# Where a matmul's moving operand starts in a 512-byte row: shifted x operands in a retention and two-MLP kernel

## The chip, the core and the metric

The kernel runs on one core of a Trainium2 chip. The core has a matrix engine (TensorE, PE in the rows, with its weight loads as PEld), a vector engine (VectorE, DVE), a scalar engine (ScalarE, ACT), a general engine (GpSimd, POOL), a queue engine that issues the DMAs here (SyncE, SP), an on-chip memory SBUF of 128 partitions, and PSUM, where matmuls put their sums. The metric is device time of one launch in microseconds (us); less is better.

## What is computed

Retention (attention without softmax, with a decay per head) over 4 batches, 8 heads, 576 positions and 64 dimensions; its output, 2304 tokens of 512 numbers, goes through two MLPs with a hidden width of 2048. All in float32.

```
scores = scale * np.matmul(q, k.transpose(0, 1, 3, 2))
Dmat = np.where(rel >= 0, gamma[:, None, None] ** rel[None, :, :], 0.0)
x = np.matmul(scores * Dmat, v)                  # -> [2304, 512]
h = np.maximum(x @ w_in, 0.0);  x = h * h @ w_out            # first MLP
h = x @ w_in2;  g = h * np.clip(h + 3.0, 0.0, 6.0) / 6.0     # second MLP
out = g @ w_out2
```

## The kernel before

To keep float32 accuracy on a faster matmul type (F32R), every operand is split in a high part and a low rest, and each product is three matmuls: high x high, low x high, high x low. A matmul has a stationary operand (the weights, 128 columns that are loaded into the array first) and a moving operand (its columns stream through). Every matmul of the MLPs has its own weight load.

**First MLP (0 to about 452 us).** The tokens are cut in five blocks of 512, 384, 512, 384 and 512 (`BLOCKS`, L30). A block's x, both parts, is one SBUF tile made by `new_x` (L696): the 512-token blocks 0, 2 and 4 take it from the pool `xapool`, blocks 1 and 3 from `xbpool`. For each block the loop `steps` goes over 16 slices f of the hidden width: `h_part` (L611) does 12 matmuls with weights w and moving operand x (L623), ScalarE and VectorE square the positive part into g, and `a_part` (L645) does 12 matmuls with weights w and moving operand g (L660). Between them stand small matmuls of the retention, which makes the x of later blocks. The weights of all 16 slices stay in SBUF, in the pools `wlo` and `whi`. In the background the second MLP's weights are read, combined, split and written to DRAM (`unit_work`).

**Second MLP (about 452 us to the end).** It uses a seven-product scheme for 2 x 2 blocks of matrices, so its operands are sums and differences, seven of each, named q in the order `ORDER` = 1, 6, 7, 5, 2, 4, 3. The tokens are cut in three passes of 768 (two halves of 384). The seven x operands `x_ops[q]` are SBUF tiles from pool `p1a`, made by `x_tiles` (L791) and filled for each pass by `x_stages`. Weights come from DRAM through a ring of seven SBUF tiles (`ring_load`, L937): six lie in `p1a`, every seventh in `p1c`. Each pass has two layers:

- first layer, L1183: for 8 slices j and 7 operands q, 6 matmuls of 384 columns. Weights: the ring tile. Moving: `x_ops[q]`. 336 matmuls a pass.
- second layer, L1238: for 7 operands q and 8 slices k, 9 matmuls of 256 columns. Weights: the split activation `spl`, one of six tiles, filled by `a_cast` (L1109) and `a_low`. Moving: the ring tile. 504 matmuls a pass. Five of the `spl` tiles lie in `p1a`; the first is a part of an older tile of `upool`, from column `FIRST_SHIFT` on (L1106, L1115).

The order on each engine is written out: in the first MLP by the loop, in the second by a list of due times (`at` and `run`) that only sets the order of issue. What each instruction waits for follows from its tiles.

Where a tile starts in SBUF follows from what its pool has handed out before. `p1a.tile([P, SHIFT])` on L1107 is 64 bytes that nobody uses, ahead of the `spl` tiles; `align` (L108) is another such tile; L1255 fills up behind.

Of the kernel before, what the change touches and what calls it, by code (L numbers as in the profile page):

```python
# [11 lines left out]
F32 = mybir.dt.float32  # L12
F32R = mybir.dt.float32r
# [6 lines left out]
P = 128  # L20
# [5 lines left out]
NC = DM // P  # L26
NF = DFF // P
NCHUNK = NT // P

BLOCKS = [(512, "xa"), (384, "xb"), (512, "xa"), (384, "xb"), (512, "xa")]  # L30


# [2 lines left out]
SUPERS, HALF = 3, 384  # L35
# [51 lines left out]
def retention_moe_kernel(ctx: ExitStack, tc, qk, kv, w1, w2, cst, out):  # L87
# [5 lines left out]
    nc = tc.nc  # L93
    nblk = len(BLOCKS)
    start = np.concatenate([[0], np.cumsum([n for n, _ in BLOCKS])]).tolist()

    def pool(stack, name, bufs, **kw):
        return stack.enter_context(tc.tile_pool(name=name, bufs=bufs, reuse_waits="tile", **kw))
# [97 lines left out]

    n0 = BLOCKS[0][0] // P
    ch = {}
    xs = {}
# [411 lines left out]
    def h_part(ph, blk, f, between=lambda: None):  # L611
        nb = BLOCKS[blk][0]
        w = wts[ph, f, 0]
        x = xs[ph, blk]
        hp = ps_h.tile([P, 512], F32, tag="h", name=f"h_{ph}_{blk}_{f}")
        def order(last):
            return [(c, wi, xi) for wi, xi in ((0, 0), last[::-1], last) for c in range(NC)]

        parts = 2 if ph == blk == f == 0 else 1
        for i in range(parts):  # L620
            ts = slice(i * nb // parts, (i + 1) * nb // parts)
            for k, (c, wi, xi) in enumerate(order((1, 0) if blk == 0 and i == 0 else (0, 1))):
                nc.tensor.matmul(  # L623
                    hp[:, ts],
                    w[:, wi, c * P : (c + 1) * P],
                    x[:, xi, c, ts],
                    start=k == 0,
                    stop=k == 3 * NC - 1,
                )
        r = tmpp.tile([P, 512], F32, tag="tmp", name=f"r_{ph}_{blk}_{f}")  # L630
        r = r[:, :nb]
        nc.scalar.activation(r, hp[:, :nb], AF.Relu)  # L632
        between()
        nc.vector.tensor_tensor(r, r, hp[:, :nb], ALU.mult)  # L634
        g = gpool.tile([P, 2, 512], F32R, tag="g", name=f"g_{ph}_{blk}_{f}")
        nc.scalar.activation(g[:, 0, :nb], r, AF.Copy)  # L636
        gts[ph, blk, f] = g, r

    def g_low(ph, blk, f):
        g, r = gts[ph, blk, f]  # L640
        nb = BLOCKS[blk][0]
        nc.vector.tensor_tensor(g[:, 1, :nb], r, g[:, 0, :nb].bitcast(F32), ALU.subtract)  # L642
        gts[ph, blk, f] = g

    def a_part(ph, blk, f):  # L645
        nb = BLOCKS[blk][0]
        w = wts[ph, f, 1]
        g = gts.pop((ph, blk, f))
        if f == 0:
            two = [  # L650
                ps_acc.tile([P, 2, 512], F32, tag="acc", name=f"acc_{ph}_{blk}_{d}")
                for d in range(2)
            ]
            accs[ph, blk] = [two[d // 2][:, d % 2, :] for d in range(NC)]
        acc = accs[ph, blk]
        last = f == NF - 1

        def mm(d, wi, gi, first, stop):
            wt = w[:, wi, d * P : (d + 1) * P]
            nc.tensor.matmul(acc[d][:, :nb], wt, g[:, gi, :nb], start=first, stop=stop)  # L660

        if last:
            for d in range(NC):
                mm(d, 0, 0, False, False)
                mm(d, 1, 0, False, False)
                mm(d, 0, 1, False, True)
        else:
            for d in range(NC):
                mm(d, 0, 0, f == 0, False)
                mm(d, 1, 0, False, False)  # L670
            for d in range(NC):
                mm(d, 0, 1, False, False)

    p1a = None
# [21 lines left out]
    def new_x(ph, blk):  # L696
        nb, tag = BLOCKS[blk]
        p = xbpool if tag == "xb" else xapool
        xs[ph, blk] = p.tile([P, 2, NC, nb], F32R, tag=tag, name=f"x_{ph}_{blk}")

# [85 lines left out]
    x_ops = {}  # L788
    xpre = None

    def x_tiles(p):  # L791
        for q in ORDER:
            x_ops[q] = p.tile([P, 2, 2, HALF], F32R, tag=f"x{q}", name=f"xop_{q}")

    def x_stages(s):

# [65 lines left out]
    for f in range(2, 4):  # L862
        load_w(0, f)
    nc.sync.dma_start(con, cst[:, DK0:])
    new_x(0, 0)

    first_q(0, nc.vector)
# [98 lines left out]
    for i, (ph, blk, f) in enumerate(steps):  # L966
# [38 lines left out]
        if blk + 1 < nblk:  # L1005
            if f == 0:
                new_x(0, blk + 1)
# [5 lines left out]
        if i == half:  # L1013

            right.close()
            p1a = xpre = pool(ctx, "p1a", 1, side="right")
            x_tiles(p1a)
            x_first = x_stages(0)
            for st in x_first:
                do(st[0])  # L1020
# [35 lines left out]
    def run(t):  # L1056
        while heap and heap[0][0] <= t:
            _, _, fn, a = heapq.heappop(heap)
            fn(*a)  # L1059
# [43 lines left out]

    SHIFT, FIRST_SHIFT = 64 // 4, 192 // 4  # L1106
    p1a.tile([P, SHIFT], F32, tag="shift0", name="shift0")  # L1107

    def a_cast(s, q, k):  # L1109
# [51 lines left out]
    for s in range(SUPERS):  # L1161
# [8 lines left out]
        for j in range(NJ):  # L1170
# [5 lines left out]
            for i, q in enumerate(ORDER):  # L1176
                run(now)
                w = wring[s, 0, j, i // 2][:, i % 2]
                x = x_ops[q]
# [72 lines left out]
            if q not in to:  # L1252
                at(now, merge, q, *{1: (s1, None), 6: (u2, s1), 7: (u3, u2)}[q])
    run(1e9)
    p1a.tile([P, 128 - SHIFT], F32, tag="shift1", name="shift1")  # L1255


# [35 lines left out]
```

## Time and profile before

| | before |
|---|---|
| time, median of 2 runs | 804.15 us (803.68 and 804.63) |
| span of the profiled execution | 802.6 us |
| TensorE busy | 796.4 us, 99% |
| VectorE, ScalarE, GpSimd busy | 592, 398, 168 us |
| first MLP with retention, about | 0 to 452.8 us |
| second MLP: first layers, three stretches | 58.3, 58.2 and 58.3 us |
| second MLP: second layers, three stretches | 57.2, 57.3 and 57.3 us |

The rows come from one profiled execution. Busy time of an engine is the union of its instructions' times; matmuls overlap, each lasting longer than the step from one start to the next, so the step is read from a run of them: the length of the run, without the last one's own duration, over the count less one. In the chain (the work that ended last, followed back from the end) each piece runs from the end of the piece ahead, and its length over its count is the step.

### The profile page before, as it was taken

What the parts mean: (1) busy time and instruction counts of PE and PEld (TensorE: products, weight loads), DVE (VectorE), ACT (ScalarE), POOL (GpSimd) and SP (SyncE); (2) the same over time, 40 slices, a digit from 0 to 9 for tenths busy, and PEclk for the clock granted to TensorE, in tenths of its full rate; (3) what the DMA queues carried; (4) which work ended last, traced back from release to release, by engine and by line L of the source; (5) the groups of instructions that cost most, each with busy time, mean ns of one, the idle gap of its engine ahead of it and who ended that gap; (6) DMA issues with size and microseconds to landing.
All of it is one profiled execution on the core that took longest, in us unless ns stands there. A gap on an engine that the chain in (4) does not pass through costs nothing.

```text
span 802.6 us, 16522 instructions
## 1 busy us (share of the span) xinstructions
PE 796.4 (99%) x6380; PEld 741.0 (92%) x6380; DVE 591.9 (74%) x1086; ACT 397.5 (50%) x738; POOL 167.7 (21%) x161
## 2 busy tenths in 40 slices
PE   8999999999999999999999999999999999999998
PEld 8788889999888899998888899999999999999998
DVE  5989987887755577776557867997577987677864
ACT  2797745444443444444435533666234655244553
POOL 4412130211011011100000065500255500256300
PEclk9999999999999999999999999999999999999999
DMA  9957626777756487856448797888887979877884
GB/s 331 352 189 248 223 93 203 225 214 222 222 157 184 124 260 212 234 158 184 145 130 269 242 303 256 306 307 291 274 264 242 353 261 302 279 240 266 272 274 139
DMA packets 148494, 189.64 MB, mean 236 GB/s; under 512 B 22592, under 2 KB 102080, under 8 KB 148416
## 3 DMA queue, kind: packets, MB, share of 16 engines
q1 hardware_dynamic: 148416, 188.59, 73.5%
q8 instruction: 50, 0.82, 0.4%
q14 instruction: 28, 0.23, 0.1%
HBM read 149.76 MB, written 38.80 MB: 235 GB/s over the span
## 4 chain that ended last, share of the span: by engine, by line
PE 95%; DMA 3%; DVE 1%; SPq 0%; ACT 0%; issue 0%; DVEq 0%
PE acc L660 24%; PE h L623 24%; PE z L1183 22%; PE z L1238 21%; PE at L496 2%; DMA raw<-w_dram 1%; DMA v<-kv_dram 1%; DMA kv<-kv_dram 1%; PE alone L496 0%; PE sc L408 0%; PE o L459 0%; PE sc L419 0%; DVE wt L158 0%; DVE wt L159 0%; PE o L469 0%; ACT w L167 0%
## 5 line engine op out<-in xcount | busy, mean ns | idle before, releaser
L660 PE MATMUL acc<-g,w 128*128 128x512 f32 (+1 forms) x960 | 213.3, 370 | 0.4 <-ACT g L636 0.4
L623 PE MATMUL h<-x,w 128*128 128x512 f32 (+2 forms) x972 | 210.6, 365 | 0.2 <-ACT w L167 0.2
L660 PEld LDWEIGHTS acc<-g,w 128*128 128x128 f32 x960 | 173.6, 188 | 25.2 <-ACT g L636 0.8
L623 PEld LDWEIGHTS h<-x,w 128*128 128x128 f32 x972 | 175.7, 188 | 22.8 <-ACT w L167 0.6
L1183 PE MATMUL z<-xop,ring 128*128 128x384 f32 x1008 | 175.2, 334 | 0.0
L1183 PEld LDWEIGHTS z<-xop,ring 128*128 128x128 f32 x1008 | 174.7, 188 | 0.1
L1238 PE MATMUL z<-ring,spl 128*128 128x256 f32 x1512 | 172.2, 276 | 0.0
L1238 PEld LDWEIGHTS z<-ring,spl 128*128 128x128 f32 x1512 | 172.1, 188 | 0.0
L1099 POOL TENSOR_TENSOR aop<-aop,aop 128x384 f32<-128x384 f32 x96 | 106.2, 1116 | 296.2 <-DVE aop L1096 292.4
L1121 DVE TENSOR_TENSOR spl<-aop,spl 128x384 fp32r<-128x384 f32 x168 | 100.5, 617 | 30.7 <-ACT spl L1117 29.4
L1117 ACT ACTIVATE spl<-aop 128x384 fp32r<-128x384 f32 x168 | 86.3, 523 | 54.7 <-PE z L1238 49.8
L632 ACT ACTIVATE r<-h 128x512 f32<-128x512 f32 (+1 forms) x80 | 44.3, 553 | 110.7 <-PE h L623 110.4
L1093 ACT ACTIVATE aop<-held,small 128x384 f32<-128x384 f32 x72 | 44.4, 617 | 108.4 <-DVE held L1059 107.8
L634 DVE TENSOR_TENSOR r<-r,h 128x512 f32<-128x512 f32 (+1 forms) x80 | 50.5, 632 | 53.9 <-ACT r L632 53.5
L1059 DVE TENSOR_TENSOR held<-z,held 128x384 f32<-128x384 f32 x120 | 66.4, 553 | 28.9 <-PE z L1183 26.7
L636 ACT ACTIVATE g<-r 128x512 fp32r<-128x512 f32 (+1 forms) x80 | 47.2, 590 | 65.8 <-DVE r L634 65.8
L642 DVE TENSOR_TENSOR g<-r,g 128x512 fp32r<-128x512 f32 (+1 forms) x80 | 54.7, 684 | 21.0 <-ACT g L636 18.5
L1096 DVE SCALAR_TENSOR_TENSOR aop<-aop,held 128x384 f32<-128x384 f32 x72 | 49.9, 692 | 17.7 <-ACT aop L1093 16.1
L393 POOL TENSOR_TENSOR qs<-qs,con 128x512 f32<-128x512 f32 x11 | 14.7, 1340 | 136.3 <-DMA qs<-qk_dram 123.9
L750 ACT ACTIVATE uhi<-seven 128x896 fp32r<-128x896 f32 x32 | 30.6, 955 | 23.7 <-DVE seven L740 14.0
L755 DVE TENSOR_TENSOR seven<-seven,uhi 128x896 fp32r<-128x896 f32 x32 | 34.9, 1089 | 7.3 <-ACT uhi L750 7.0
L174 POOL TENSOR_TENSOR w<-wt,w 128x512 fp32r<-128x512 f32 x17 | 22.7, 1336 | 62.9 <-ACT w L167 60.2
(111 smaller groups left out, 609.8 us busy)
## 6 DMA issues: line engine op xcount, KB each, us to landing
ring<-w_out_hl SPq DMA_DIRECT2D x84, 512.0 KB, 4.9
ring<-w_in_hl SPq DMA_DIRECT2D x72, 512.0 KB, 4.7
raw<-w_dram SPq DMA_DIRECT2D x32, 512.0 KB, 7.1
uraw<-w_dram SPq DMA_DIRECT2D x64, 256.0 KB, 3.2
q<-qk_dram SPq DMA_DIRECT2D x17, 512.0 KB, 5.3
w_in_hl<-uhi SPq DMA_DIRECT2D x16, 448.0 KB, 3.4
w_in_hl<-seven SPq DMA_DIRECT2D x16, 448.0 KB, 4.8
w_out_hl<-uhi SPq DMA_DIRECT2D x16, 448.0 KB, 3.2
```

Source lines behind the costliest of these rows:

```text
L623: nc.tensor.matmul(hp[:, ts], w[:, wi, c * P : (c + 1) * P], x[:, xi, c, ts], start=k == 0, stop=k == 3 * NC - 1,)
L634: nc.vector.tensor_tensor(r, r, hp[:, :nb], ALU.mult)
L636: nc.scalar.activation(g[:, 0, :nb], r, AF.Copy)
L642: nc.vector.tensor_tensor(g[:, 1, :nb], r, g[:, 0, :nb].bitcast(F32), ALU.subtract)
L660: nc.tensor.matmul(acc[d][:, :nb], wt, g[:, gi, :nb], start=first, stop=stop)
L1059: fn(*a)
L1096: stt(f32(q, j), f32(q, j), 6.0, h, ALU.min, ALU.mult)
L1099: nc.gpsimd.tensor_tensor(f32(o, j), f32(a, j), f32(b, j), op)
L1117: act(t[:, 0, :], f32(q, k), AF.Copy)
L1121: tt(t[:, 1, :], f32(q, k), t[:, 0, :].bitcast(F32), ALU.subtract)
L1183: nc.tensor.matmul(bank[q], w[:, wi, u * P : (u + 1) * P], x[:, u, xi, :], start=k == 0 and q not in (2, 4, 3), stop=k == 5, skip_group_ch ...
L1238: nc.tensor.matmul(o, sp[:, g, P * n : P * (n + 1)], w[:, k % 2, wi, :], start=k == 0 and m == 0 and n % 2 == 0 and q not in (2, 4, 3), st ...
```

## The change

Nothing is computed differently. Tiles get unused elements, so that operands start at other places in SBUF:

- the x tile of blocks 0, 2 and 4 becomes 128 elements (512 bytes) longer, and x starts in it at element 0, 8 or 120 (`X_PLACE`), which is 0, 32 or 480 bytes on;
- each of the seven x operands of the second MLP becomes 8 elements (32 bytes) longer, so that each starts 32 bytes further in a row of 512 bytes than the one before it, and everything behind them in `p1a` moves by 224 bytes;
- `FIRST_SHIFT` grows by the same 224 bytes, and the filler at the end shrinks by it.

```
+X_PLACE = {0: 0, 2: 8, 4: 120}
     def new_x(ph, blk):
         nb, tag = BLOCKS[blk]
         p = xbpool if tag == "xb" else xapool
-        xs[ph, blk] = p.tile([P, 2, NC, nb], F32R, tag=tag, name=f"x_{ph}_{blk}")
+        n = 2 * NC * nb
+        if tag == "xa":
+            t = p.tile([P, n + P], F32R, tag=tag, name=f"x_{ph}_{blk}")
+            t = t[:, X_PLACE[blk] : X_PLACE[blk] + n]
+            xs[ph, blk] = t.rearrange("p (x c t) -> p x c t", x=2, c=NC)
+        else:
+            xs[ph, blk] = p.tile([P, 2, NC, nb], F32R, tag=tag, name=f"x_{ph}_{blk}")
     def x_tiles(p):
         for q in ORDER:
-            x_ops[q] = p.tile([P, 2, 2, HALF], F32R, tag=f"x{q}", name=f"xop_{q}")
+            t = p.tile([P, 4 * HALF + 8], F32R, tag=f"x{q}", name=f"xop_{q}")
+            x_ops[q] = t[:, : 4 * HALF].rearrange("p (u x t) -> p u x t", u=2, x=2)
-    SHIFT, FIRST_SHIFT = 64 // 4, 192 // 4
+    SHIFT, FIRST_SHIFT = 64 // 4, (192 + 224) // 4
-    p1a.tile([P, 128 - SHIFT], F32, tag="shift1", name="shift1")
+    p1a.tile([P, 128 - SHIFT - 56], F32, tag="shift1", name="shift1")
```

The places below are those of the two built programs: the start address in a partition, modulo 512 bytes. All matmul operands inside one tile start whole multiples of 512 bytes apart, so a tile has one place. Distance is the weights' place less the moving operand's, modulo 512; a distance of 480 is one of 32 bytes the other way.

| matmuls | operands | before: weights, moving | distance | after: weights, moving | distance |
|---|---|---|---|---|---|
| L623, blocks 0, 1, 3 (588) | w, x | 160, 160 | 0 | 160, 160 | 0 |
| L623, block 2 (192) | w, x | 160, 160 | 0 | 160, 192 | 480 |
| L623, block 4 (192) | w, x | 160, 160 | 0 | 160, 128 | 32 |
| L660 (960) | w, g | 160, 160 | 0 | 160, 160 | 0 |
| L1183, ring slots 0 to 5 (870) | ring, x of q = 1, 6, 7, 5, 2, 4, 3 | 160, 160 | 0 | 384; 160, 192, 224, 256, 288, 320, 352 | 224, 192, 160, 128, 96, 64, 32 |
| L1183, ring slot 6 (138) | the same | 160, 160 | 0 | 160; the same | 0, 480, 448, 416, 384, 352, 320 |
| L1238, slots 0 to 5 (1296) | spl, ring | 224 or 352, 160 | 64 or 192 | 448 or 64, 384 | 64 or 192 |
| L1238, slot 6 (216) | spl, ring | 224 or 352, 160 | 64 or 192 | 448 or 64, 160 | 288 or 416 |

In L1238 one weights tile in six is the one at 352 (64 after). Over all of L1183 the distances after are 0 for 18 matmuls, 32 for 126, 480 for 18, and 64 or more either way for 846.

The order of the instructions on all five engines is the same in both programs, row for row. Of what they wait for, one thing differs: before, GpSimd's first operation on the activations of the second MLP (L1099) waits for ScalarE, which had used the SBUF under that tile; after, it doesn't.

## Rows read from the trace of the kernel before

**Rows 1.** The page's first lines: span; busy us, share of the span, instructions.

```profile
span 802.6 us, 16522 instructions
...
PE 796.4 (99%) x6380; PEld 741.0 (92%) x6380; DVE 591.9 (74%) x1086; ACT 397.5 (50%) x738; POOL 167.7 (21%) x161
```

**Rows 2.** The page's chain that ended last: shares of the span by engine, by line.

```profile
PE 95%; DMA 3%; DVE 1%; SPq 0%; ACT 0%; issue 0%; DVEq 0%
PE acc L660 24%; PE h L623 24%; PE z L1183 22%; PE z L1238 21%; PE at L496 2%; DMA raw<-w_dram 1%; DMA v<-kv_dram 1%; DMA kv<-kv_dram 1%; PE alone L496 0%; PE sc L408 0%; PE o L459 0%; PE sc L419 0%; DVE wt L158 0%; DVE wt L159 0%; PE o L469 0%; ACT w L167 0%
```

**Rows 3.** All waits of TensorE: who waited for whom, us in total, times, longest.

```profile
PE unread L851 <- POOL early L845: 1.0, 1, 1.0
PE o L292 <- POOL v L267: 0.5, 1, 0.5
PE o L292 <- POOL kv L267: 0.4, 1, 0.4
PE acc L660 <- ACT g L636: 0.4, 1, 0.4
PE o L302 <- POOL states L348: 0.2, 1, 0.2
PE h L623 <- ACT w L167: 0.2, 1, 0.2
```

**Rows 4.** Chain in order of time, first MLP: start, us, what; blocks 1, 2, 3/4.

```profile
148.46 2.08 PE h L623 x12
150.54 2.08 PE acc L660 x12
...
247.78 2.72 PE h L623 x12
250.50 2.72 PE acc L660 x12
...
366.14 2.10 PE acc L660 x12
368.24 2.76 PE h L623 x12
```

**Rows 5.** The same chain, second MLP: three passes of two layers.

```profile
452.82 58.27 PE z L1183 x336
511.09 57.18 PE z L1238 x504
568.27 58.24 PE z L1183 x336
626.51 57.32 PE z L1238 x504
683.83 58.25 PE z L1183 x336
742.08 57.25 PE z L1238 x504
```

**Rows 6.** Timeline of TensorE in three stretches: start, us from first start to last end.

```profile
23.03 2.44 PE L623 MATMUL h<-x,w 128*128 128x256 f32 x19
...
626.35 5.34 PE L1238 MATMUL z<-ring,spl 128*128 128x256 f32 x44
...
631.41 52.42 PE L1238 MATMUL z<-ring,spl 128*128 128x256 f32 x461
```

**Rows 7.** One line's instructions: duration of one in ns, min/median/max, and forms.

```profile
L623 PE MATMUL h<-x,w x972: 281/389/504, 22.7 to 446.8; 128*128 128x512 f32 x113, 128*128 128x384 f32 x77, 128*128 128x256 f32 x5
...
L1238 PE MATMUL z<-ring,spl x1512: 276/276/285, 510.9 to 799.0; 128*128 128x256 f32 x189
```

**Rows 8.** Busy us by stretch: span, PE, PEld, DVE, ACT, POOL, clock, DMA share, GB/s.

```profile
453.00:511.00 58.00, 58.00 (x336) 58.00 (x336) 44.22 (x77) 23.21 (x46) 29.32 (x28) 1.00 0.86 280
511.00:568.00 57.00, 57.00 (x505) 57.00 (x504) 47.05 (x90) 34.53 (x72) 5.03 (x5) 1.00 0.89 307
```

**Rows 9.** Ring loads of the second layers (L947): from issue to landing.

```profile
DMA to landing us min/median/max: 3.9/4.9/8.9
```

## Prediction, made before the run

> **What bounds the kernel now.** I read the page's busy list and its chain first. TensorE (PE) is busy 796.4 of 802.6 us [rows 1] and the chain that ended last runs over it for 95%, nearly all of it in four lines: the two matmul lines of the first MLP (L660, L623) and the two of the second (L1183, L1238) [rows 2]. The view of waits leaves no other candidate: TensorE's longest wait is 1.0 us, at the start, and the next that belongs to an MLP is 0.4 us [rows 3]. So nothing is to be had by feeding TensorE earlier. What counts is the time from one matmul to the next while it is fed without a gap.
>
> That time is in the chain, piece by piece. In the first MLP twelve matmuls of 512 columns take 2.72 us and twelve of 384 columns 2.08 us, L623 and L660 alike [rows 4]: 226.7 and 173.3 ns each. The difference, 53.3 ns for 128 columns, is one column per cycle of the 2.4 GHz level. At that rate 512 columns are 213.3 ns and 384 are 160.0, so either width carries the same surcharge of 13.3 ns. L1183, also 384 columns wide, takes 58.24 us for 336, again 173.3 ns [rows 5]. L1238, 256 columns wide, is different: the row of 461 takes 52.42 us; without the last one's own 0.276 us [rows 7] that is 52.14 / 460 = 113.35 ns [rows 6], and 256 columns are 106.7. Its surcharge is 6.7 ns, half of the others'. A narrower matmul alone does not explain it: L623's own 256-column matmuls in block 0 take (2.44 - 0.28) / 18 = 120.0 ns [rows 6, 7], the full 13.3.
>
> What sets L1238 apart is where its operands lie. By the table of places in the section on the change, in L623, L660 and L1183 the weights and the moving operand start at the same place of a 512-byte row (distance 0), in L1238 they start 64 or 192 bytes apart. I read the 6.7 ns as the price of distance 0: the load of the next weights runs beside the current matmul and both walk their rows in step. The rows show the price; the cause is an inference.
>
> **The change, part by part.** No instruction is added, removed or reordered; one wait of GpSimd on ScalarE, before its first L1099, drops out because tiles overlap other tiles. GpSimd is busy 29.3 of 58 us there [rows 8] and no wait of TensorE names it in the second MLP [rows 3]: nothing.
>
> *x of the second MLP (L1183).* Of the 1008 matmuls 18 stay at distance 0. 846 get a distance of 64 bytes or more either way. The nearest rows are L1238's at 64 and 192: its chain pieces of 504 contain 84 at distance 192 and still average 57.25 / 504 = 113.6 ns [rows 5], so both distances cost the same 6.7. I take that: 846 x 6.67 ns = **5.64 us** gained. The other 144 get a distance of 32 bytes one way or the other, halfway between a row that costs 13.3 and one that costs 6.7; I take the middle, 10.0: 144 x 3.33 = **0.48 us**. Bounds for both: 0 and 990 x 6.67 = 6.60 us.
>
> *x of blocks 2 and 4 (L623).* 2 x 16 x 12 = 384 matmuls of 512 columns, at distances of 480 and 32. Again the middle: 384 x 3.33 = **1.28 us**; bounds 0 and 2.56. L660 between them keeps distance 0 and gains nothing.
>
> *Changes of distance.* L1183 now changes distance at every operand, each six matmuls. L1238 changes between 64 and 192 at every sixth piece of nine matmuls and averages no more for it, so I take nothing. The bound: alternating widths at a block's end cost 2.76 instead of 2.72 us per twelve [rows 4], 0.04 us; over the 64 changes between L623 and L660 in blocks 2 and 4 that would be 2.6 us, which eats that part's best gain.
>
> *Weights and pieces of the second layer (L1238).* Ring slots 0 to 5 move 224 bytes and the pieces with them, so 1296 matmuls keep their 64 or 192. Slot 6 lies in another pool and stays: its 216 get 288 or 416. The nearest row is that of 192: nothing. Bounds: all 216 at 13.3 lose 1.4 us; no row has less than 6.7.
>
> *Who must keep up.* If L1183 runs at 166.7 ns, its stretch shrinks by 4%. VectorE is busy 44.2 of 58 us there and DMA engines 0.86 [rows 8], which become 0.79 and 0.89; the second layer runs its DMA at 0.89 now without a wait. A ring tile lands 8.9 us after its issue at worst [rows 9]; L1183 spends four tiles on 42 matmuls, 7.28 us, so the other six slots give some 6 x 1.82 = 10.9 us between issue and use, and 10.5 after the change. The cover holds.
>
> **The sum.** 5.64 + 0.48 + 1.28 = 7.40 us, all on the path, since TensorE waits for nobody. The profiled execution spans 802.6 us [rows 1]; 795.2 follows. The median of the runs is 804.15, 1.55 above that span, and I carry this over: **796.8 us**. With every moved x at 6.7 ns it is 804.15 - 9.16 = 795.0; with half of the first term and nothing else 804.15 - 2.8 = 801.3. That is the forecast's own range.
>
> A rule speaks against all of this. The rows show the same shape, 256 columns, at 120.0 and at 113.35 ns [rows 6]. The Trainium skill (TensorE: Matmul & The Clock Gate, Step-by-step: what each phase is for) holds that TensorE has two independent SBUF read ports, one for the moving operand and one for the weight load, and that loading the next weights takes no read bandwidth from the running matmul; by that rule a place in SBUF is worth nothing and the time would stay at 804.15. The trace agrees that loads run beside matmuls without a visible wait, not that all pairs cost the same.
>
> **The rivals.**
>
> *A, the forecast:* distance 0 costs one 6.7 ns step, other distances don't. 796.8.
>
> *B, the place is not the cause.* L1238 also differs from L1183 in who wrote its operands (its moving operand comes by DMA, its weights from ScalarE and VectorE; in L1183 it is the other way) and in the order of its loads, and the 120.0 ns row is only 24 matmuls at the program's start. Then nothing moves: **804.2**. The port rule above is this rival. Against it: 120.0 and 113.35 are exact and steady, at one width.
>
> *C, slower: the pair falls out of step.* Distance is not all. After the switch from L1183 the row of 44 L1238 matmuls takes (5.34 - 0.28) / 43 = 117.7 ns at the very distance 64 that later takes 113.35 [rows 6]. The start of a run decides, and it can last. Slot 6 now breaks the pattern every seventh tile. If that puts all 1512 on 117.7, they lose 1512 x 4.35 = 6.6 us; and if the 990 moved L1183 matmuls sit as high, at 11.0 ns over their columns, they gain only 990 x 2.3 = 2.3, with nothing from L623: 804.15 + 4.3 = **808.5**. It ends slower as soon as L1238's loss exceeds what L1183 gains.
>
> *D, a second gain: 64-byte pieces.* 6.7 ns at 2.4 GHz is 16 columns, 64 bytes of a row. All operands stand at 160 now, 2.5 such pieces, so 256 columns touch 17 pieces instead of 16; 17 x 6.67 is 113.3, L1238's time exactly. After the change x of blocks 2 and 4 (384), three of the seven x operands (432) and ring slots 0 to 5 as moving operand (1296) start on a multiple of 64. If each lost a piece: 2112 x 6.67 = 14.1 us on top of 9.16, **780.9**. For it: the exact fit. Against it: no row of any start on a multiple of 64, and a fixed 6.7 ns per matmul fits as well. The Trainium skill (the same page, Back-to-back issue gap) gives columns over 2.4 GHz plus 2.5 ns for a lone gap, 162.5 for 384; no matmul of this trace comes that low, and the 1374 moved x matmuls there would bring an estimate of 789.3.
>
> **Chances and range.** A 0.66, B 0.14, C 0.10, D 0.10. The likeliest is 796.8. Within 2%, about what a measurement of this kernel can tell from no change, means 788.1 to 820.2: A, B and C lie inside, D below. So faster 0.10, same 0.89, slower 0.01. The range leaves out C above and D below, 2 in 10 together: it reaches up to B, 804.5, and down halfway from the forecast's 795.0 to D, 788.0.
>
> **What would show it.** In the chain, the three L1183 pieces of 336 fall from 58.25 us to between 56.0 (166.7 ns) and 56.7; the twelves of L623 fall from 2.72 to 2.64 or 2.68 in blocks 2 and 4 and stay in block 0; L660 stays at 2.72; the L1238 pieces stay at 57.2. Unchanged L1183 pieces mean B. L1238 above 58 means C; L1238 under 56 means D, and then L1183 differs between its operands by their start. L623 differing between block 2 (480) and block 4 (32) tells which of the two is good. A new wait of TensorE on a ring tile's DMA would mean that the cover was thinner than worked out.

## The result: 7.5 us slower

| | before | after |
|---|---|---|
| time, median | 804.15 us | 811.64 us (811.03 and 812.25) |
| ratio, 95% interval | | 1.0092 [1.0063, 1.0121] |
| span of the profiled execution | 802.6 us | 810.4 us |
| start of the second MLP in the chain | 452.8 us | 456.7 us |

The change was forecast to save 7.4 us and cost 7.5. The lines of the changed file stand a little lower: L624 is L623 of before, L661 is L660, L1191 is L1183, L1246 is L1238.

TensorE still bounds the kernel, and no matmul of the MLPs waits for anything that it didn't wait for before. Of the page after, the span and the busy times, and of TensorE's eight waits the three longest:

```profile
span 810.4 us, 16522 instructions
...
PE 803.9 (99%) x6380; PEld 745.5 (92%) x6380; DVE 592.1 (73%) x1086; ACT 398.1 (49%) x738; POOL 169.4 (21%) x161
```

```profile
PE unread L859 <- POOL early L853: 1.0, 1, 1.0
PE o L293 <- POOL kv L268: 0.6, 1, 0.6
PE acc L661 <- ACT g L637: 0.4, 1, 0.4
```

TensorE is busy 7.5 us longer and waits little more than in [rows 3]: the eight waits come to 3.2 us, the six before to 2.7, and what has been added lies in the retention at the start. The same matmuls take longer. Where, the chain after shows (start, us, what): first block 2, then block 4, then the second MLP.

```profile
249.31 2.80 PE h L624 x12
252.11 2.76 PE acc L661 x12
...
403.86 2.80 PE h L624 x12
406.66 2.75 PE acc L661 x12
...
456.68 58.91 PE z L1191 x336
515.59 57.82 PE z L1246 x504
573.41 58.91 PE z L1191 x336
632.33 58.03 PE z L1246 x504
690.35 58.90 PE z L1191 x336
749.25 57.93 PE z L1246 x504
```

Block 4 before, of which [rows 4] have only the start:

```profile
400.93 2.72 PE h L623 x12
403.65 2.72 PE acc L660 x12
```

Against these and [rows 4] twelve L623 take 0.08 us more in both shifted blocks, and the untouched twelve L660 beside them 0.03 to 0.04 more: 32 x 0.08 + 32 x 0.035 = 3.7 us. Against [rows 5] the three L1183 pieces take 0.64, 0.67 and 0.65 us more, the three L1238 pieces 0.64, 0.71 and 0.68: 4.0 us. Together 7.7 of the 7.8 us between the spans. So the loss has four places, all of them on the path, and none is a gain.

### The profile page after: what moved, and what is told of

It reads as the page before. It is cut to its first block, busy times and chain, and to the rows that moved or that the text cites. A ratio compares the mean times of both kernels' runs of the same rounds, so it can differ in the third digit from the quotient of the medians.

```text
span 810.4 us, 16522 instructions
## 1 busy us (share of the span) xinstructions
PE 803.9 (99%) x6380; PEld 745.5 (92%) x6380; DVE 592.1 (73%) x1086; ACT 398.1 (49%) x738; POOL 169.4 (21%) x161
## 4 chain that ended last, share of the span: by engine, by line
PE 95%; DVE 2%; DMA 1%; SPq 1%; ACT 1%; issue 0%; POOL 0%; DVEq 0%; POOLq 0%
PE acc L661 24%; PE h L624 24%; PE z L1191 22%; PE z L1246 21%; PE at L497 2%; DMA q<-qk_dram 1%; DVE wt L159 1%; PE alone L497 0%; DVE wt L160 0%; PE sc L409 0%; ACT w L168 0%; PE o L460 0%; PE sc L420 0%; PE o L470 0%; POOL q L264 0%
## 5 line engine op out<-in xcount | busy, mean ns | idle before, releaser
L661 PE MATMUL acc<-g,w 128*128 128x512 f32 (+1 forms) x960 | 213.8, 371 | 0.4 <-ACT g L637 0.4
L624 PE MATMUL h<-x,w 128*128 128x512 f32 (+2 forms) x972 | 213.1, 368 | 0.2 <-ACT w L168 0.2
L624 PEld LDWEIGHTS h<-x,w 128*128 128x128 f32 x972 | 175.7, 188 | 24.8 <-ACT w L168 0.6
L661 PEld LDWEIGHTS acc<-g,w 128*128 128x128 f32 x960 | 173.7, 188 | 26.0 <-ACT g L637 0.8
L1191 PE MATMUL z<-xop,ring 128*128 128x384 f32 x1008 | 177.2, 337 | 0.0
L1191 PEld LDWEIGHTS z<-xop,ring 128*128 128x128 f32 x1008 | 176.6, 188 | 0.1
L1246 PE MATMUL z<-ring,spl 128*128 128x256 f32 x1512 | 174.3, 278 | 0.0
L1246 PEld LDWEIGHTS z<-ring,spl 128*128 128x128 f32 x1512 | 174.2, 188 | 0.0
```

What stands on the lines that cost most here:

```text
L624: nc.tensor.matmul(hp[:, ts], w[:, wi, c * P : (c + 1) * P], x[:, xi, c, ts], start=k == 0, stop=k == 3 * NC - 1,)
L1191: nc.tensor.matmul(bank[q], w[:, wi, u * P : (u + 1) * P], x[:, u, xi, :], start=k == 0 and q not in (2, 4, 3), stop=k == 5, skip_group_ch ...
L1246: nc.tensor.matmul(o, sp[:, g, P * n : P * (n + 1)], w[:, k % 2, wi, :], start=k == 0 and m == 0 and n % 2 == 0 and q not in (2, 4, 3), st ...
```

## The experiments

Each is the kernel before with an edit, unless it says otherwise. The times stand against runs of the kernel before on the same chip (804.3 to 804.4 us).

### The two halves of the change apart

Only `X_PLACE` and `new_x` of the change:

```
+X_PLACE = {0: 0, 2: 8, 4: 120}
```

> Only the x of blocks 2 and 4 is shifted (distances 480 and 32); the second MLP is the kernel before's. The changed kernel's trace puts twelve L623 of these blocks at 2.80 us instead of 2.72 and twelve L660 beside them at 2.75. Theory P (each pair of places has its own price and the parts add up): 32 pieces x (0.08 + 0.03) = +3.5 us against before, about 807.7; the second MLP's pieces stay at 58.25 and 57.25. Rival G (the loss is one of the whole kernel, such as shifted buffers or DMA): no more than 1 us of it shows here.

Only `x_tiles`, `FIRST_SHIFT` and the filler:

```
+            t = p.tile([P, 4 * HALF + 8], F32R, tag=f"x{q}", name=f"xop_{q}")
...
+    SHIFT, FIRST_SHIFT = 64 // 4, (192 + 224) // 4
...
+    p1a.tile([P, 128 - SHIFT - 56], F32, tag="shift1", name="shift1")
```

> Only the second MLP is changed (seven x operands 32 bytes further each, the rest moved by 224 bytes); the blocks are the kernel before's. Theory P: L1183's pieces of 336 take 58.9, L1238's pieces of 504 take 57.9, together +3.9 us, about 808.1; the first MLP is as before. Rival G: under 1 us.

The first came to 807.46 us, ratio 1.0039 [1.0025, 1.0054], the second to 808.66 us, 1.0050 [1.0035, 1.0065]: +3.1 and +4.3 us, 7.4 together against 7.5 for the whole. The parts add up, so each can be looked at by itself, and a loss of the whole kernel is out.

### Does the distance matter at all?

```
-    SHIFT, FIRST_SHIFT = 64 // 4, 192 // 4
-    p1a.tile([P, SHIFT], F32, tag="shift0", name="shift0")
+    SHIFT, FIRST_SHIFT = 0, 0
```

> The 64 unused bytes ahead of the activation pieces and the 192 in the first of them are taken out of the kernel before, so that L1238's weights and moving operand stand at distance 0 as in L1183. Theory P, as the prediction had it (distance 0 costs 13.3 ns, other distances 6.7): a matmul goes from 113.35 to 120.0 ns, a piece of 504 from 57.25 to 60.5, the time to about 814. Rival R (L1238 is cheaper for its width, its order or the writers of its operands, not for its distance): the pieces stay at 57.2 and the time at 804.

814.19 us, ratio 1.0122 [1.0107, 1.0137]. Its chain, two pieces of the second MLP (L1182 and L1237 are L1183 and L1238 of before):

```profile
571.37 58.24 PE z L1182 x336
629.62 60.47 PE z L1237 x504
```

60.47 / 504 = 120.0 ns instead of 113.4 to 113.7 [rows 5]. Same matmuls, same writers, same order; only the weights' tiles have moved by 64 or 192 bytes. Rival R, which is the prediction's B, is out: the place changes the time of a matmul, and for L1238 distance 0 is the dear one, as the prediction read it.

### The good distances of L1238, given to L623

x of blocks 0, 2 and 4 at distances 448, 64 and 192 (`new_x` as in the change):

```
+X_PLACE = {0: 16, 2: 112, 4: 80}
```

> x of blocks 0, 2 and 4 at distances 448, 64 and 192 from its weights; all else is the kernel before's. Theory P (64 and 192 are good distances wherever they stand, only 32 either way is bad): twelve L623 fall to 2.64 us in blocks 2 and 4, about -2.5 us for the two. Rival L (L623 runs in step at distance 0 and any other distance breaks it): 2.80 us in all three blocks, +0.08 x 48 = 3.8 us, with L660 beside it another 1.5.

808.30 us, ratio 1.0047 [1.0032, 1.0062]. Its chain in block 2 (distance 64), then block 4 (192):

```profile
252.49 2.74 PE acc L661 x12
255.24 2.80 PE h L624 x12
...
401.24 2.77 PE acc L661 x12
404.01 2.76 PE h L624 x12
```

At 64, where L1238 pays least, L623 takes 233.3 ns, 6.7 more than at 0; at 192 it takes 230. Neither theory had it quite: 192 is milder than 64, but every distance tried here is worse than 0. What is good at 256 columns is bad at 512.

### A bench: price by width and distance

Matmuls alone, 48 in a series, at 16 distances:

```
for p, ds in (("a", range(0, 512, 32)), ("b", range(480, -1, -32))):
    for n in (256, 384, 512):
        for d in ds:
            run(f"n{n}d{d}{p}", n, [(0, d)] * 48)
...
run("sixesa", 384, [(0, d) for d in range(224, 0, -32) for _ in range(6)] * 4)
...
run("twelvesa", 512, [(0, d) for d in (32, 0) for _ in range(12)] * 5)
...
```

> A bench of matmuls alone, each with its own weight load: it leaves the whole computation out, and writes zeros. Weights stand at 160 of a 512-byte row; series of 48 matmuls of 256, 384 and 512 columns go through all 16 distances in steps of 32 bytes, up (a) and down (b), then with the weights at 192 in steps of 64 (h); then series that change distance on the way (sixes: every 6 matmuls as L1183 now does; twelves: every 12, as L623 and L660; nines: as L1238 before, and with 288 in it). Theory P (distance alone sets the price): at each width 13.3 ns over the columns at distance 0, 6.7 at 64 and 192. Theory W (width and distance together): 256 columns as just said, 512 columns 13.3 at 0 and 20.0 at 32, 64 and 480; 384 columns unknown, and the uniform series tell whether L1183's 175.5 ns come from its distances or from the changes between them (sixes alone at 175).

Rows of its chain; the name holds columns, distance and direction (a up, b down, h up with the weights at 192):

```profile
32.92 5.75 PE n256d0a L115 x48
...
44.35 5.66 PE n256d64a L115 x48
...
67.16 5.45 PE n256d192a L115 x48
...
78.21 5.75 PE n256d256a L115 x48
...
112.45 5.45 PE n256d448a L115 x48
...
486.88 5.66 PE n256d192b L115 x48
...
123.51 8.33 PE n384d0a L115 x48
...
165.27 8.48 PE n384d160a L115 x48
...
635.65 8.38 PE n384d64b L115 x48
...
257.60 10.88 PE n512d0a L115 x48
268.48 11.20 PE n512d32a L115 x48
...
324.49 11.00 PE n512d192a L115 x48
...
844.71 5.46 PE n256d64h L115 x48
...
855.87 5.65 PE n256d192h L115 x48
...
1039.48 29.44 PE sixesa L115 x168
...
1098.18 27.73 PE twelvesa L115 x120
1125.91 27.80 PE twelvesb L115 x120
1153.71 25.44 PE ninesa L115 x216
1179.15 25.17 PE ninesb L115 x216
```

A row over its count, less the columns at 2.4 GHz, is the surcharge. In ns, up and down series:

| distance | 256 columns | 384 columns | 512 columns |
|---|---|---|---|
| 0 | 13.1, 13.1 | 13.5, 14.0 | 13.3, 13.5 |
| 32 | 11.7, 11.7 | 13.8, 14.0 | 20.0, 19.8 |
| 64 | 11.2, 11.0 | 13.1, 14.6 | 19.8, 19.8 |
| 96 | 12.1, 11.9 | 13.5, 13.8 | 21.0, 20.8 |
| 128 | 11.9, 12.1 | 16.0, 16.0 | 19.4, 20.0 |
| 160 | 13.1, 13.1 | 16.7, 16.7 | 20.0, 20.2 |
| 192 | 6.9, 11.2 | 13.3, 13.3 | 15.8, 15.8 |
| 224 | 10.2, 11.2 | 16.7, 13.3 | 19.8, 20.0 |

In the up series distances of 256 and more repeat the table from 0 (256 as 0, 448 as 192) within 0.02 us a row, in the down series within 0.06. With nothing else running on the core, distance 0 costs 13.1 to 14.0 ns at all three widths, as in the kernel (13.3), and 32 at 512 columns the 233.3 ns of L623 after the change. Theory P is out: the price of a distance differs with the width. At 512 columns 0 is the best place; at 384 nothing is more than 0.7 ns better than 0, and 128, 160 and, in the up series, 224 are worse by about 3; only at 256 does a distance help. But Theory W had 6.7 for 256 columns at 64, and these series give 11.

So width and distance are not all of it. With the weights at 192 instead of 160, 256 columns are cheap at 64 and not at 192, the other way round than in the up series (5.46 and 5.65 us against 5.66 and 5.45); these series step by 64, so each also has another one ahead of it. And the nines, which give L1238's sequence of distances to the bench, do not behave as L1238 does: 25.44 / 216 = 117.8 ns throughout, where L1238 takes 113.4, and with two of six pieces at 288 they get faster, 116.5, where L1238 got slower. The bench differs from L1238 in the places themselves (weights at 160, in L1238 at 224 and 352) and in the order of its slices; which of these counts, no series separates.

The sixes run through L1183's seven distances as after the change: 29.44 / 168 = 175.2 ns, the kernel's 58.91 / 336 = 175.3. The mean of the seven up series is 174.7. So of the 2.0 ns that L1183 lost per matmul, about 1.4 are the distances themselves and 0.5 the changes between them. The twelves between 32 and 0 come to 231.1 where the mean of their two series is 230.0, those between 480 and 0 to 231.7: going back and forth costs 1.1 and 1.8 ns per matmul, or 0.026 and 0.042 us for twelve of either kind together. L660 lost 0.03 us per twelve between L623 at 32 (block 4) and 0.04 at 480 (block 2), so this is about what it lost for its neighbours' sake.

### No path of distances is cheaper

A second bench changes the distance from matmul to matmul:

```
...
run(f"n{n}x{step}a", n, [(0, step * k % 256) for k in range(64)])
...
run(f"n{n}p{step}a", n, [(0, step * (k % 2)) for k in range(64)])
...
```

> A second bench of matmuls alone (it leaves the computation out and writes zeros): series of 64 at 256, 384 and 512 columns whose distance changes in a fixed way. x: the moving operand walks back by 32 to 224 bytes with every matmul (modulo 256); w: the weights walk on by as much; p: every other matmul at that distance, the rest at 0; q: two and two. The first bench found 13.3 ns as the least for 384 and 512 columns at any one distance, 6.7 only for 256. Theory T (the price belongs to the path of distances, as a state that carries from matmul to matmul; a walk can hold the cheap state at any width): some walk at 384 or 512 columns settles at 6.7 ns, which over 2940 matmuls of the kernel would be worth up to 19.6 us. Rival F (at 384 and 512 columns 13.3 is the floor): no series at these widths comes below 13; then distance 0, the kernel before's, is the best place for L623, L660 and L1183, and the change had nothing to gain there.

Its two shortest series at 384 and 512 columns:

```profile
467.53 11.10 PE n384p224a L115 x64
...
779.70 14.52 PE n512p64a L115 x64
```

173.4 and 226.9 ns: 13.4 and 13.5 over the columns. None of the 28 series at either width is below 13. In this range of paths Rival F holds. At 256 columns none came below 10.0 (7.47 us for 64), so no path tried holds the cheap state there either.

### L1238: the seventh tile

The second MLP's change alone, with slot 6 of the ring moved like the others:

```
+    p1c.tile([P, 56], F32, tag="shift2", name="shift2")
```

> The second MLP's change alone, with 224 unused bytes ahead of ring slot 6 in its own pool as well, so that slot 6 has the places of the other six slots: L1238 is back at distances 64 and 192 throughout, L1183 runs through 224 to 32 with every tile. Theory S (L1238 lost because slot 6 at 288 and 416 puts it out of step, which lasts until the next tile at 192): its pieces of 504 come back from 57.9 to 57.25, and the time falls by 2.0 us against the second MLP's change alone (808.7 to 806.7). Rival M (L1238 lost because everything moved from 160 to 384): the pieces stay at 57.9.

806.25 us, ratio 1.0026 [1.0015, 1.0036], 2.4 us under the second MLP's change alone. Its chain:

```profile
453.17 58.93 PE z L1185 x336
512.10 57.18 PE z L1240 x504
...
628.21 57.13 PE z L1240 x504
```

L1238 is back at its old length, with its operands at 384 and 448 instead of 160 and 224. So all it had lost, it lost to slot 6. How, the timeline of the changed kernel shows (start, us, count), in three stretches at distance 64 throughout: behind a tile of slot 6 whose two pieces stood at 416 and 288, some microseconds later, and behind the next tile of slot 6, whose two pieces both stood at 288:

```profile
536.22 4.05 PE L1246 MATMUL z<-ring,spl 128*128 128x256 f32 x33
...
542.76 5.83 PE L1246 MATMUL z<-ring,spl 128*128 128x256 f32 x50
...
551.49 1.41 PE L1246 MATMUL z<-ring,spl 128*128 128x256 f32 x11
```

(4.05 - 0.28) / 32 = 117.8 ns, then (5.83 - 0.28) / 49 = 113.3. Between them the weights tile at distance 192 came by, and the step is restored behind it. In the third stretch it is (1.41 - 0.28) / 10 = 113.0 again within a few matmuls, though no tile at 192 has come by. So the cheap state of 256 columns has to be held: a tile of slot 6 ends it, and whether 64 alone brings it back depends on what ran before.

### The prediction's main term by itself

All seven x operands at distance 64, no changes between them:

```
     def x_tiles(p):
+        p.tile([P, 112], F32, tag="shift2", name="shift2")
         for q in ORDER:
             x_ops[q] = p.tile([P, 2, 2, HALF], F32R, tag=f"x{q}", name=f"xop_{q}")
+        p.tile([P, 16], F32, tag="shift3", name="shift3")
```

> The kernel before with 448 unused bytes ahead of the seven x operands and 64 behind them: all of L1183 at distance 64, no change of distance inside a pass; all else as before. The prediction's main term (what L1238 pays at 64, L1183 pays too): its pieces of 336 fall from 58.25 to 56.0, the time by 6.7 us to 797.6. Theory W (width and distance together, as the bench gave them: 384 columns at 64 settle at 13.3, or at 14.5 where the run starts badly): the pieces take 58.25 to 58.65, the time stays at 804 to 805.5.

805.98 us, ratio 1.0020 [1.0011, 1.0028]. Its chain:

```profile
453.63 58.69 PE z L1185 x336
512.32 57.40 PE z L1240 x504
569.73 58.68 PE z L1185 x336
```

Of its timeline, the start of the first L1238 piece:

```profile
512.63 6.64 PE L1240 MATMUL z<-ring,spl 128*128 128x256 f32 x55
```

58.69 / 336 = 174.7 ns, the 14.6 over the columns of the down series at 64; the piece and the time lie just above Theory W's range. The term that was to bring 6.7 us if given to all of L1183 loses 0.43 x 3 = 1.3. The first L1238 piece, whose places in the row are unchanged, takes 57.40 us instead of 57.18: it starts at (6.64 - 0.28) / 54 = 117.8 ns, and its first tile, which stands at 192, does not restore the step here. A tile at 192 is thus no sure remedy.

### Starting each second layer in step

```
-        n = len(splits) % NSPL
+        n = len(splits) % (7 * NJ) % NSPL
```

> The kernel before with the six activation tiles counted anew in each pass, so that every second layer starts with the tile at distance 192. Theory S (a run that is out of step at 117.8 ns comes into step at 113.3 with the next tile at 192, which in passes 2 and 3 comes only after 36 and 18 matmuls): the L1238 pieces of passes 2 and 3 fall from 57.32 and 57.25 to 57.18, the time by 0.2 us. Rival: they stay, and what ended the 117.8 ns was something else. Either way the time itself can't show it; the pieces can.

804.39 us, ratio 0.9999 [0.9990, 1.0008]. Its chain:

```profile
626.08 57.18 PE z L1238 x504
...
741.50 57.19 PE z L1238 x504
```

57.32 and 57.25 of [rows 5] became 57.18 and 57.19, as far as the theory of the lost step said. That is 0.2 us, which no time of this kernel can show; it is the only thing found that the kernel before leaves lying here.

## Why the prediction was wrong, step by step

- **What bounds the kernel: right.** Of the 7.8 us between the spans 7.7 are matmuls that follow each other more slowly; no wait was added in the MLPs, and the ring kept up.
- **"L1238 is apart by the place of its operands": right,** and now shown rather than inferred: distance 0 makes it 120.0 ns. Rival B is out, and with it what the prediction drew from a rule, that a place in SBUF is worth nothing: 64 or 192 bytes of it were worth 6.7 ns of 120.0. The rule itself, of the Trainium skill (TensorE: Matmul & The Clock Gate, Step-by-step: what each phase is for), is that a weight load takes no read bandwidth from the running matmul; no run here shows whether it does.
- **"The nearest rows are L1238's at 64 and 192 ... I take that" for L1183: this step failed,** and with it 5.64 of the 7.40 us. It carried a price from 256 columns to 384. The prediction had tested whether width alone explains the rows, and found it doesn't; it never tested whether distance alone does. The bench at 384 columns has no distance more than 0.7 ns below distance 0, and some that are 3 above it. Alone at 64, L1183 takes 174.7 ns, where 166.7 were counted on; the seven distances bring 175.3.
- **"Halfway", 10.0 ns for distances of 32 either way: failed, at 512 columns with its sign.** There the price is 20.0, outside the two rows between which it was interpolated; at 384 columns the bench has 13.8 to 14.0 at 32, no gain either. The bound below, "0 and 2.56 us" gained, excluded a loss without a reason: no row of 512 columns away from distance 0 stood behind it.
- **Changes of distance, taken at nothing: too small.** By the bench they cost L1183 some 0.5 ns a matmul, 0.5 us in all, and in the kernel L660 about 1.1 us. The bound given, 2.6 us from the rows of alternating widths, held them.
- **L1238's slot 6, taken at nothing with a bound of 1.4 us: failed; 2.0 us.** The bound counted slot 6's own 216 matmuls and not those behind it that run out of step at the old distance.
- **Rival C had that mechanism,** from the row at 117.7 ns, and the time came out 3 us above its 808.5. It overstated L1238 (6.6 us for 2.0, since the step comes back, mostly behind a tile at 192) and still let L1183 gain 2.3, where it lost 2.0, and L623 and L660 none, where they lost 3.7.
- **Rival D, 64-byte pieces: out.** With moving operand and weights on multiples of 64, L1238 takes the same 113.4 ns (57.18 / 504). Its premise was not exact either: not all operands stood at 160 before, L1238's weights stood at 224 and 352.

What stays open is why. The runs show prices, a state that is carried from matmul to matmul, and a repeat when the moving operand is moved by 256 bytes; they don't show which access waits for which, nor why L1238's distances are cheap at its own places and not in the bench's nines. No series without weight loads was tried, so the load beside the matmul is still an inference.

## What to carry to other kernels

A price read from one shape of matmul holds for that shape: before carrying it to another width, look for a row of that width, and where there is none let the range include a loss. Where TensorE already ran back to back, the places of weights and moving operand were worth 6.7 ns of 120.0 at 256 columns and 6.7 of 226.7 at 512, and the same distance, 64, was good at 256 columns and among the worst at 512. A bench of short series gave the prices at 384 and 512 columns in one run; at 256 it did not reproduce the kernel, so there the place has to be tried in the kernel itself. Where distances differed between neighbours, the matmuls behind a change paid too.

## What the runs showed of the hardware that was not expected

- The step from one F32R matmul with its own weight load to the next depends on the places of both operands, and a move of the moving operand by 256 bytes changed little or nothing: at 256 columns, going up, 5.75 us for 48 at distances 0 and 256, 5.45 at 192 and 448. The distance alone does not fix it: with the weights at 192 instead of 160, the cheap distance was 64 (5.46 us) and not 192 (5.65).
- It has a memory. The same 48 matmuls at distance 192 took 5.45 us coming from 160 and 5.66 coming from 224; in the kernel 117.8 and 113.3 ns stand side by side at distance 64.
- At 384 and 512 columns no distance and no path tried brought the surcharge below 13 ns; at 256 columns it can be 6.7. Per column, 256 in step (113.3 ns) and 512 at distance 0 (226.7 ns) cost the same.
